# The first 256 tokens of a max-of-three layer begun while the attention of the next 256 is prepared

## The chip, the cores and the metric

One core of a Trainium2 chip runs the kernel. The engines are TensorE (PE; its weight loads are listed apart as PEld), VectorE (DVE), ScalarE (ACT), GpSimd (POOL) and SyncE (SP, which here issues most of the DMAs). The metric is the device time of one launch in microseconds (us), the median of several runs.

## The reference

Linear attention with a decay per step feeds a layer that takes the largest of three products and multiplies by a fourth matrix. Four batches, 8 heads, 768 steps, head size 48; 3072 tokens, model width 384, inner width 768.

```python
def _attn_ref(r, k, v, w, u):
    state = np.zeros((B, H, D, D)); y = np.zeros_like(r)
    for t in range(S):
        cur = np.einsum('bhd,bhe->bhde', u[None] * kt, vt)
        y[:, :, t] = np.einsum('bhd,bhde->bhe', rt, state + cur)
        state = wt[:, :, :, None] * state + np.einsum('bhd,bhe->bhde', kt, vt)
    return y

def _moe_ref(x, w1, w2, w3, w_out):
    h = np.maximum(np.maximum(x @ w1, x @ w2), x @ w3)
    return h @ w_out
```

## The kernel before

The attention runs in 24 chunks of 128 steps, numbered through the batches, six to a batch. The layer runs in six halves of 512 tokens, so four chunks feed one half. The steps of a chunk k have one letter each, and a table of such letters sets the order in which they are written into the engines' queues; every engine then works strictly in that order, and waits with everything behind it when an operand is missing.

- **b, f**: two scans on DVE over the decays (L324, L334); two short operations stand ahead of f (L332, L333). **r**: two multiplications on DVE that apply the scans to the keys and queries in `tin` (L345, L344). **c**: a check on ACT.
- **d, e**: the diagonal term of the first eight chunks: a multiplication on DVE into `kr` (L356), four small products on PE (L369, written as part of e), a copy of their sums to SBUF on DVE (`cs`, L371), and a select on POOL that spreads them into `a` (L376).
- **X**: the scores on PE (L394). **M**: two masked copies on DVE that take the scores into `a` (L401). **T**: transposes on PE (L411), copied by ACT into `kn`.
- **R, V**: products on PE with the state (L424) and the values (L458) into `y`. **E**: ACT copies `y` into `x` (L467). **U**: products on PE for the next state (L434, for chunks 1 to 3 also L438). **S**: its scaling on DVE (L449).
- **n**: the load of `tin` of a chunk (SP). **w**: the load of one of the 24 weight tiles (SP). **W**: products on zeros on PE, which have no reader (L490).

After E of the last chunk of a half, six small DMAs copy rows inside `x` (L472), three from each of SP and ACT for half 0, and six from SP for the later halves. Only then can the half's products start. The weights arrive in 64 bits and are turned into fp32 by one ACT operation (L268) and two on DVE (L277, L279) for each of the 24 tiles, the "conversion" below. Half 0 is "plain": it multiplies fp32 tiles as they are. The later halves split `x` and the weights into two parts and make three products of each.

A half has 18 column groups, three (one of each weight matrix) for each 128 columns of the inner width. A group is three 128x512 matmuls in PSUM (L146). ACT copies the first of three groups to SBUF, and DVE takes the maximum with the second and third (L128). The string `START` sets how groups (m), attention steps (a), conversions (c) and splits (f) alternate until half 1 begins; after that a rule in the main loop does. Every DMA issue waits until the one eight issues earlier has landed.

Of the kernel before, what the change touches and what calls it, by code (L numbers as in the profile page):

```python
# [42 lines left out]
NP = 4  # L43
# [23 lines left out]
FRONT = "w U0 b1 | d1 f1 r1 | w e1 c1 S0 W2 X1 T1 | R0 M0 | V0 E0 n3 |"  # L67
LAST = "w R0 M0 | V0 E0 U0 W9 n3 | b1 d1 | f1 r1 w | e1 c1 S0 X1 T1 R1 |"
TURN = "b1 d1 w | f1 w | r1 c1 | e1 M0 w | "
ORD = "w R0 X1 U0 V0 E0 b2 d2 | f2 n3 w | S0 r2 c2 | e2 M1 w | T1 w | |"  # L70


START = ("aaaaaaaaaaaacaaacaccaxmcacmcamcamcamcamcamcamcamcaamca"
         "mcmacamcacammacmcamacamcamcamcamcamcaafafafaxmafmmammaaf")
# [15 lines left out]
def kernel(ctx: ExitStack, tc, tin, nat, u_flat, u_pair, v_t, w_all, out, ytr):  # L90
# [21 lines left out]

    def moe_groups(x_hi, x_lo, pools, store):

        plain = x_lo is None
        ps_m, hp, mp = pools
        h_hi, h_lo, later, behind = [], [], [], []
        top = {}  # L120

        def take_up(wi, ps):
            if wi == 0:
                top["m"] = hp.tile([128, HT], F32, name="h_hi") if plain else mp.tile([128, HT], F32, name="m")
                nc.scalar.copy(out=top["m"][:, :], in_=ps[:, :])
                return
            m = top["m"]
            nc.vector.tensor_tensor(out=m[:, :], in0=ps[:, :], in1=m[:, :], op=ALU.max)  # L128
            if wi == 2 and plain:
                h_hi.append(m)  # L130
            elif wi == 2:
# [20 lines left out]
        flush(behind)  # L152
        flush(later)
        order = []
        for tt in range(CPH):
            order += [(tt, f) for f in range(FT - 1)]
            order += [(tt - 1, FT - 1)] if tt else []
        order.append((CPH - 1, FT - 1))
        pss = {}
        for n, (tt, f) in enumerate(order):  # L160
            if f == 0:
                pss[tt] = ps_m.tile([128, HT], F32, name="psm")
# [12 lines left out]
    with ExitStack() as fast:  # L175
# [23 lines left out]
        def load_nat(k):  # L199
            b, c = divmod(k, NCH)  # L200
            vt = v_p.tile([128, DM], F32, name="v")
            kr = nat_p.tile([128, 2, DM], F32, name="kr")
            if k >= CS:
                nc.sync.dma_start(out=kr[:, :, :], in_=nat[b, c, :, 1:3, :])
            nc.sync.dma_start(out=vt[:, :], in_=nat[b, c, :, 0, :])
            natt[k] = (vt, kr)
# [108 lines left out]
        load(1)  # L315
        load(2)
        u_bc = cst.tile([128, DM], F32, name="u_bc")
# [34 lines left out]
        def prep_diag1(k):  # L352
            n = natt[k][1]
            if k < CS:
                t = tbuf[k % NB]
                nc.vector.tensor_tensor(out=n[0:112, :, :].rearrange("p a b -> p (a b)")[:, 0:NP * C],  # L356
                                        in0=t[0:112, WC:WC + NP * C], in1=t[0:112, WC + NP * C:TC_], op=ALU.mult)
                return
            nc.gpsimd.tensor_tensor(out=n[:, 0, :], in0=n[:, 0, :], in1=n[:, 1, :], op=ALU.mult)
            nc.gpsimd.tensor_tensor(out=n[:, 0, :], in0=n[:, 0, :], in1=u_bc[:, :], op=ALU.mult)  # L360

        def prep_diag2(k):
            n = natt[k][1]
            cs = small.tile([128, LINE], F32, name="cs")[:, 0:H]
            if k < CS:
                t = tbuf[k % NB]
                ps = ps_m.tile([128, HT], F32, name="psm")
                for pr in range(NP):
                    nc.tensor.matmul(ps[:, 2 * pr:2 * pr + 2], lhsT=n[0:112, :, :].rearrange("p a b -> p (a b)")[:, pr * C:(pr + 1) * C],  # L369
                                     rhs=t[0:112, TC_ + 2 * pr:TC_ + 2 * pr + 2], start=(pr == 0), stop=(pr == NP - 1))  # L370
                nc.vector.tensor_copy(out=cs[:, :], in_=ps[:, 0:H])  # L371
            else:
                nc.vector.tensor_reduce(out=cs[:, :], in_=n[:, 0, :].rearrange("p (h d) -> p h d", h=H),  # L373
                                        axis=AX.X, op=ALU.add)
# [10 lines left out]
        def scores(k):  # L385

            p = prep[k]
            spare = k < CPH and k % 2
            p["gs"] = gs = [ps_m.tile([128, NP, C], F32, name="psm") if spare else ps_g.tile([128, NP, C], F32, name="gram")
                            for _ in range(2)]  # L390
# [70 lines left out]
        def result(k):  # L461
# [12 lines left out]
        steps = dict(X=scores, M=take, T=transposes, R=from_state, U=to_state, S=state, V=values, E=result, n=load,  # L474
                     b=prep_scan_b, f=prep_scan_f, r=prep_rk, c=prep_check, d=prep_diag1, e=prep_diag2)
# [11 lines left out]
        def warmer(n):  # L487
            wps = ps_m.tile([128, HT], F32, name="psm")
            for _ in range(n):
                nc.tensor.matmul(wps[:, :], lhsT=warm[:, :], start=True, stop=True,  # L490
                                 rhs=warm[:, :].unsqueeze(1).broadcast_to([128, HT // 128, 128]))

        def attn():
            for step in "bdfeWrXTcW":
                ahead(step, 0) if step != "W" else warmer(2 if ("X", 0) in ready else 8)
            for k in range(NK):
                if k == CPH:
                    nc.scalar.dma_start(out=u_bc[:, :], in_=u_flat.partition_broadcast(128))
                for step in (FRONT if k < CPH - 1 else LAST if k < CPH else TURN + ORD if k == CPH else ORD).split():
# [4 lines left out]
                    elif step[0] == "W":  # L504
                        warmer(int(step[1]))
                    else:
                        ahead(step[0], k + int(step[1]))

        def x_parts(half):
            x = xt.pop(half)  # L510
            if half < PLAIN:
                return x, None
# [14 lines left out]
        done = fixed = 0  # L527

        def weights():

            nonlocal done
            if done > NW:
                return
            while loaded < min(NW, done + NST):
                load_w()
            if done < NW:
                split_w1(done)
            if done >= 1:
                split_w2(done - 1)
# [13 lines left out]
        units = groups = 0  # L553
# [34 lines left out]

        def group():
            nonlocal groups, mg  # L590
            half = groups // GPH
            if groups % GPH == 0:
# [3 lines left out]

                def store(tt, o):
                    nc.sync.dma_start(out=out[half * HT + tt * C:half * HT + (tt + 1) * C, :], in_=o)

                mg = moe_groups(*xs[half], pools, store)  # L600
            g = groups % GPH
            while done < 1 + (NW if half or g >= 3 * FT else g + 1):
# [10 lines left out]

        for step in START:
            if step == "a":
                unit()
            elif step == "c":
                weights()
# [4 lines left out]
            else:  # L623
                group()
# [163 lines left out]
```

## Time and profile before

| | us |
|---|---|
| median of three runs | 432.44 (430.42 to 436.3) |
| the profiled execution, its own time | 429.81 |
| span of its trace | 428.1 |

The trace covers 428.1 us of the profiled execution's 429.81 us. In the trace PE is the engine with the longest busy time, and nearly all of its idle time lies in the first 40 us. A fp32 matmul stands in the trace as two PE instructions.

### The profile page before, as it was taken

How to read it: one execution, taken by the hardware profiler on the slowest of the kernel's cores; microseconds unless marked ns; L12 is line 12 of the kernel's file. 1: busy time of each engine (PE TensorE's matmuls, PEld its weight loads, DVE VectorE, ACT ScalarE, POOL GpSimd, SP SyncE). 2: the span in 40 equal slices, each digit the busy share in tenths (PEclk: the TensorE clock that was granted, in tenths of full speed). 3: DMA queues.
4: the chain of work that ended last, by engine and by line, in shares of the span. 5: the costliest groups of instructions: out<-in, count | busy, mean ns of one | idle time of the engine just before them, and what ended most of it. 6: DMA issues, size and time to landing. Idle time of an engine off the chain costs nothing.

```text
span 428.1 us, 7355 instructions
## 1 busy us (share of the span) xinstructions
PE 414.1 (97%) x2921; PEld 324.8 (76%) x2921; DVE 275.6 (64%) x483; ACT 152.4 (36%) x318; POOL 64.4 (15%) x67
## 2 busy tenths in 40 slices
PE   6998999999999999999999999999999999999994
PEld 2774555546678888988888978888988888988893
DVE  6999779788759968747758458758547623233310
ACT  1353424142534534425334445434623321312211
POOL 3120111030333021112103112202112100000000
PEclk9899999999999999999999999999999999999998
DMA  8868935443280412294643494662360000200001
GB/s 218 262 183 246 319 88 167 115 144 93 67 255 13 122 39 83 48 311 161 195 147 122 143 314 140 190 195 75 103 231 2 0 2 2 93 2 0 1 21 61
DMA packets 20701, 53.22 MB, mean 124 GB/s; under 512 B 2816, under 2 KB 9088, under 8 KB 20656
## 3 DMA queue, kind: packets, MB, share of 16 engines
q1 hardware_dynamic: 16832, 42.61, 32.6%
q10 hardware_dynamic: 3824, 10.03, 7.5%
q8 instruction: 25, 0.41, 0.4%
q14 instruction: 20, 0.16, 0.1%
HBM read 46.74 MB, written 4.72 MB: 120 GB/s over the span
## 4 chain that ended last, share of the span: by engine, by line
PE 93%; DMA 3%; DVE 1%; ACT 1%; issue 1%; SPq 0%; DVEq 0%; ACTq 0%
PE psm L146 55%; PE psm L166 18%; PE y L458 6%; PE gram L394 5%; PE y L424 3%; PE tu L434 2%; PE tu L411 2%; DMA tin<-in_tin_dram 2%; PE psm L369 1%; DMA x<-x 1%; PE psm L394 1%; DVE x_lo L106 0%; DVE gf L334 0%; DVE gf L324 0%; ACT x L467 0%
## 5 line engine op out<-in xcount | busy, mean ns | idle before, releaser
L146 PE MATMUL psm<-x_hi,w 128*128 128x512 f32 x540 | 172.9, 394 | 0.0
L146 PEld LDWEIGHTS psm<-x_hi,w 128*128 128x128 f32 x540 | 101.4, 188 | 22.7 <-issue 2.1
L146 PE MATMUL psm<-x_lo,w 128*128 128x512 f32 x270 | 105.3, 390 | 0.0
L128 DVE TENSOR_TENSOR m<-psm,m 128x512 f32<-128x512 f32 x60 | 41.2, 687 | 59.6 <-PE psm L146 52.7
L166 PE MATMUL psm<-w,h_hi 128*128 128x384 f32 x288 | 78.1, 364 | 0.0
L376 POOL TENSOR_SCALAR_AFFINE_SELECT a<-cs 128x1024 f32<-128x1024 f32 x24 | 26.7, 1111 | 245.6 <-DVE cs L373 153.8
L146 PEld LDWEIGHTS psm<-x_lo,w 128*128 128x128 f32 x270 | 50.7, 188 | 10.2 <-DVE x_lo L106 0.2
L166 PEld LDWEIGHTS psm<-w,h_hi 128*128 128x128 f32 x288 | 51.8, 188 | 7.0 <-issue 1.0
L146 PE MATMUL psm<-x,w 128*128 128x512 f32 x108 | 48.3, 598 | 2.1 <-DMA x<-x 2.1
L467 ACT COPY x<-y 112x512 f32<-112x512 f32 x24 | 14.1, 587 | 77.7 <-PE y L458 77.7
L166 PE MATMUL psm<-w,h_lo 128*128 128x384 f32 x120 | 40.2, 335 | 0.0
L105 ACT CAST h_hi<-m 128x512 fp32r<-128x512 f32 x30 | 18.7, 622 | 57.6 <-DVE m L128 57.2
L146 PEld LDWEIGHTS psm<-x,w 128*128 128x128 f32 x108 | 19.9, 190 | 25.0 <-issue 22.0
L350 ACT ACTIVATE gf<-gf 112x1034 f32<-112x1034 f32 x24 | 25.6, 1069 | 34.1 <-DVE tin L345 31.4
L106 DVE TENSOR_TENSOR h_lo<-m,h_hi 128x512 fp32r<-128x512 f32 x30 | 21.9, 732 | 21.4 <-ACT h_hi L105 21.4
L324 DVE TENSOR_TENSOR_SCAN gf<-tin,d_bwd 112x517 f32<-112x517 f32 x24 | 29.5, 1228 | 7.3 <-DMA tin<-in_tin_dram 7.3
L334 DVE TENSOR_TENSOR_SCAN gf<-tin,d_fwd 112x517 f32<-112x517 f32 x24 | 29.6, 1235 | 0.8
L401 DVE COPY_PREDICATED a<-mask,gram 128x512 f32<-128x512 int32 x44 | 30.0, 736 | 0.0
L458 PE MATMUL y<-a,v 128*48 128x128 f32 (+1 forms) x384 | 27.8, 281 | 0.0
L394 PE MATMUL gram<-tin 48*128 48x128 f32 x352 | 25.6, 284 | 0.9 <-DVE tin L345 0.9
L394 PEld LDWEIGHTS gram<-tin 48*128 48x128 f32 x352 | 21.4, 187 | 6.7 <-issue 4.1
L458 PEld LDWEIGHTS y<-a,v 128*64 128x64 f32 (+1 forms) x384 | 22.2, 133 | 1.3 <-issue 0.8
(71 smaller groups left out, 420.2 us busy)
## 6 DMA issues: line engine op xcount, KB each, us to landing
tin<-in_tin_dram SPq DMA_DIRECT2D x23, 677.7 KB, 5.5
w<-in_w_all_dram SPq DMA_DIRECT2D x24, 384.0 KB, 7.7
cv<-in_w_all_dram ACTq DMA_DIRECT2D x24, 384.0 KB, 3.2
kr<-in_nat_dram SPq DMA_DIRECT2D x16, 384.0 KB, 5.7
v<-in_nat_dram SPq DMA_DIRECT2D x24, 192.0 KB, 5.2
out_dram<-m SPq DMA_DIRECT2D x24, 192.0 KB, 2.7
x<-x SPq DMA_DIRECT2D x33, 32.0 KB, 2.0
tin<-in_tin_dram SPq DMA_DIRECT2D x1, 258.0 KB, 4.4
```

What stands on the lines that cost most here:

```text
L105: nc.scalar.copy(out=hi, in_=src)
L106: rest = lambda: nc.vector.tensor_tensor(out=lo, in0=src, in1=hi.bitcast(F32), op=ALU.subtract)
L128: nc.vector.tensor_tensor(out=m[:, :], in0=ps[:, :], in1=m[:, :], op=ALU.max)
L146: nc.tensor.matmul(ps[:, :], lhsT=wt[f * 3 + wi][:, ct * 128:(ct + 1) * 128], rhs=xt[:, ct, :], start=(n == 0), stop=(n == KT * len(terms) ...
L166: nc.tensor.matmul(pss[tt][:, 0:DM], lhsT=ht[f][:, tok], rhs=wt[FT * 3 + f][:, :], start=(f == 0 and i == 0), stop=(f == FT - 1 and i == l ...
L324: nc.vector.tensor_tensor_scan(out=gf[0:112, 0, ::-1], data0=t[0:112, 0:WC][:, ::-1], data1=d_bwd[0:112, ::-1], initial=0.0, op0=ALU.mult, ...
L334: nc.vector.tensor_tensor_scan(out=gf[0:112, 1, :], data0=tbuf[k % NB][0:112, 0:WC], data1=d_fwd[0:112, :], initial=0.0, op0=ALU.mult, op1 ...
L350: nc.scalar.activation(out=flat, in_=flat, func=AF.Square, accum_out=acc[0:112, k:k + 1])
L376: nc.gpsimd.affine_select(out=a[:, :, :], in_=cs[:, :].unsqueeze(2).broadcast_to([128, H, C]), pattern=[[0, H], [1, C]], compare_op=ALU.is ...
L394: nc.tensor.matmul(gs[hh][:, pr, :], lhsT=p["kp"][q:q + 48, pr, :], rhs=p["rp"][q:q + 48, pr, :], start=(pr == 0), stop=(pr == NP - 1))
L401: nc.vector.copy_predicated(out=p["a"][:, hh::2, :], mask=mask_b(NP), data=p["gs"][hh][:, :, :])
L458: nc.tensor.matmul(p["y"][64 * half:64 * half + m, hh, j, :], lhsT=natt[k][0][:, h * D:h * D + m], rhs=p["a"][:, h, :], start=(k % NCH == ...
```

## The change

A new table `FRONT`, written out step by step with chunk numbers, replaces the tables `FRONT` and `LAST` and the beginning of `START`. It covers everything up to chunk 4.

- E of chunk 1 now starts six copies inside `x` for the first 256 tokens, three from SP and three from ACT. E of chunk 3 starts six for the other 256, all from SP.
- The nine groups of the first 384 inner columns run twice on 256 tokens (token `g` for the first time) instead of once on 512. They need chunks 0 and 1 alone.
- The conversion has two halves that the table places apart (`i` for ACT's part, `c` for both).
- The four small products of the diagonal term are a step of their own (D), and the scores of chunks 1 and 3 use the same PSUM pool as the others.
- In the front, a maximum is put into DVE's queue when the table says so (`u`) or when the third PSUM tile after it is taken; after the front, as before, one group later.
- The second chunk's values and four weight tiles are loaded earlier; products on zeros stand at other places (29 instead of 35).

The order below `START` differs until half 1 has begun; from its fifth group on PE's order is what it was.

```diff
-FRONT = "w U0 b1 | d1 f1 r1 | w e1 c1 S0 W2 X1 T1 | R0 M0 | V0 E0 n3 |"
+FRONT = ("b0 d0 D0 W6 f0 r0 X0 e0 T0 W2 c0 b1 M0 U0 R0 V0 E0 n3 i i d1 D1 W6 S0 f1 r1 e1 X1 c1 T1 R1 i "
...
+START = ("mmacmmacmmacmmacmaacmacmaacmacmaacmacmaacmacmacmaacmaacmaafxmafmmafmmaaf")
+EARLY = 3
...
+    def take_turn(pool):
+        rules["turns"] += 1
+        while held and held[0][0] <= rules["turns"] - 3:
+            held.pop(0)[1]()
+        return pool.tile([128, HT], F32, name="psm")
...
-        for f in range(FT):
+        whole, first, second = slice(0, HT), slice(0, HT // 2), slice(HT // 2, HT)
+        stretches = [(f, whole) for f in range(FT)]
+        if plain:
+            stretches = [(f, first) for f in range(EARLY)] + [(f, second if f < EARLY else whole) for f in range(FT)]
+        for f, cols in stretches:
             for wi in range(3):
                 flush(later)
-                ps = ps_m.tile([128, HT], F32, name="psm")
+                ps = take_turn(ps_m)
...
-                        nc.tensor.matmul(ps[:, :], lhsT=wt[f * 3 + wi][:, ct * 128:(ct + 1) * 128], rhs=xt[:, ct, :],
+                        nc.tensor.matmul(ps[:, cols], lhsT=wt[f * 3 + wi][:, ct * 128:(ct + 1) * 128], rhs=xt[:, ct, cols],
                                          start=(n == 0), stop=(n == KT * len(terms) - 1))
                         n += 1
-                flush(behind)
-                behind.append(lambda wi=wi, ps=ps: take_up(wi, ps))
+                while held and not rules["lazy"]:
+                    held.pop(0)[1]()
+                held.append((rules["turns"], lambda f=f, wi=wi, ps=ps, cols=cols: take_up(f, wi, ps, cols)))
                 yield
...
-            for lo in (0, 64) if slot == CPH - 1 else ():
-                for j in range(KT):
-                    eng = nc.scalar if lo and half < PLAIN else nc.sync
-                    eng.dma_start(out=x[lo + 48:lo + 64, j, :], in_=x[lo + 16 * j:lo + 16 * j + 16, KT, :])
+            early = half < PLAIN and slot == CPH // 2 - 1
+            cols = slice(HT // 2 if half < PLAIN and not early else 0, HT // 2 if early else HT)
+            for j in range(KT) if early or slot == CPH - 1 else ():
+                for lo in (0, 64):
+                    eng = nc.scalar if lo and early else nc.sync
+                    eng.dma_start(out=x[lo + 48:lo + 64, j, cols], in_=x[lo + 16 * j:lo + 16 * j + 16, KT, cols])
...
+        def early_group():
+            nonlocal ahead_by
+            if ahead_by == 0:
+                xs[0] = x_parts(0)
+                begin_half(0)
+            while done < ahead_by + 1:
+                weights()
+            next(mg)
+            ahead_by += 1
```

Three places show what moved. The first is PE where the layer starts. Names: `warm` are the zeros, `psm` a PSUM tile, `tin_114` to `tin_116` the three buffers of `tin` (chunk modulo 3). Before:

```order
L490 LDWEIGHTS warm
L490 MATMUL psm<-warm 128x512
L146 MATMUL psm<-x,w 128x512 x9
L369 MATMUL psm<-tin_115,kr 128x2 x4
L394 MATMUL gram<-tin_115 128x128 x8
L411 MATMUL tu<-ident,tin_115 128x112 x4
```

After:

```order
L520 LDWEIGHTS warm
L520 MATMUL psm<-warm 128x512
L162 MATMUL psm<-x,w 128x256 x3
L393 MATMUL psm<-tin_116,kr 128x2 x4
L162 MATMUL psm<-x,w 128x256 x6
L421 MATMUL gram<-tin_116 128x128 x8
L438 MATMUL tu<-ident,tin_116 128x112 x4
```

Before, the layer's products stand behind chunk 3 and ahead of chunk 4; now the first three groups stand ahead of the scores of chunk 2.

The second is DVE between the first scan of chunk 2 and its second. Before:

```order
L324 SCALAR_TENSOR_TENSOR gf<-tin_116,d_bwd 112x517
L356 TENSOR_TENSOR kr<-tin_116 112x512
L332 TENSOR_SCALAR d_fwd<-gf 112x4
L333 RECIPROCAL d_fwd<-d_fwd 112x4
L334 SCALAR_TENSOR_TENSOR gf<-tin_116,d_fwd 112x517
```

After:

```order
L350 SCALAR_TENSOR_TENSOR gf<-tin_116,d_bwd 112x517
L428 COPY_PREDICATED a<-mask,gram 128x4x128 x2
L298 SCALAR_TENSOR_TENSOR cv<-w,cv 128x384
L300 SCALAR_TENSOR_TENSOR w<-w,cv 128x384
L298 SCALAR_TENSOR_TENSOR cv<-w,cv 128x384
L300 SCALAR_TENSOR_TENSOR w<-w,cv 128x384
L298 SCALAR_TENSOR_TENSOR cv<-w,cv 128x384
L300 SCALAR_TENSOR_TENSOR w<-w,cv 128x384
L382 TENSOR_TENSOR kr<-tin_116 112x512
L476 TENSOR_TENSOR sstar_134<-tu,dec_136 112x4x48
L358 TENSOR_SCALAR d_fwd<-gf 112x4
```

Chunk 1's scores are now taken inside chunk 2's preparation, and three conversions stand ahead of the rest of it.

The third is SP's queue, from the load of chunk 3 on (`tin_114` for the second time). Before:

```order
L216 DMA tin_114<-in_tin_dram 112x1549
L252 DMA w<-in_w_all_dram 128x384 x2
L205 DMA v<-in_nat_dram 128x384
L216 DMA tin_115<-in_tin_dram 112x1549
L252 DMA w<-in_w_all_dram 128x384 x2
```

After:

```order
L237 DMA tin_114<-in_tin_dram 112x1549
L273 DMA w<-in_w_all_dram 128x384
L501 DMA x<-x 16x256 x3
L273 DMA w<-in_w_all_dram 128x384 x2
L237 DMA tin_115<-in_tin_dram 112x1549
```

The early copies inside `x` now stand behind one load of `tin` and one of a weight, and ahead of the next loads.

## Rows read from the trace of the kernel before

**Rows 1.** The page's busy time of PE over the span, and PE's busy tenths in 40 slices of the span.

```profile
PE 414.1 (97%) x2921; PEld 324.8 (76%) x2921; DVE 275.6 (64%) x483; ACT 152.4 (36%) x318; POOL 64.4 (15%) x67
PE   6998999999999999999999999999999999999994
```

**Rows 2.** Busy time by stretch: start and end, length, then busy us (and instructions) of PE, PEld, DVE, ACT and POOL, TensorE's granted clock, DMA share and GB/s.

```profile
0.00:38.24 38.24, 30.76 (x330) 21.64 (x330) 33.01 (x61) 14.29 (x28) 6.56 (x15) 0.96 0.77 218
38.24:421.30 383.06, 382.87 (x2591) 303.04 (x2592) 242.62 (x424) 137.12 (x288) 57.82 (x52) 1.00 0.37 116
```

**Rows 3.** The chain of work that ended last, from 0 to 140 us: start, length, engine and line. From 22.14 on it passes through chunk 2 and the diagonal term of chunk 3; at 99.36 it is in the second product of half 0 (128x384 matmuls).

```profile
22.14 1.09 PE gram L394 x16
23.23 0.54 PE tu L411 x4
23.77 0.59 PE y L424 x10
24.36 1.02 PE y L458 x15
25.38 0.45 PE tu L434 x15
25.83 0.51 PE tu L438 x2
26.34 0.79 PE psm L369 x8
...
33.34 0.59 ACT x L467
...
33.95 4.20 DMA x<-x
...
38.24 7.96 PE psm L146 x18
...
99.36 7.94 PE psm L166 x24
```

**Rows 4.** DVE in order of time: start, busy us, what. The first is chunk 0, the second chunk 1, then chunk 3 and one conversion, then the first maximum of the layer.

```profile
8.81 1.58 DVE L345 TENSOR_TENSOR tin<-tin,gf 112x512 f32<-112x512 f32 x1
10.55 1.24 DVE L324 TENSOR_TENSOR_SCAN gf<-tin,d_bwd 112x517 f32<-112x517 f32 x1 [0.16 <-DMA tin<-in_tin_dram]
...
22.92 1.23 DVE L324 TENSOR_TENSOR_SCAN gf<-tin,d_bwd 112x517 f32<-112x517 f32 x1
24.06 0.68 DVE L356 TENSOR_TENSOR kr<-tin 112x512 f32<-112x512 f32 x1
...
25.07 1.23 DVE L334 TENSOR_TENSOR_SCAN gf<-tin,d_fwd 112x517 f32<-112x517 f32 x1
26.22 0.67 DVE L344 TENSOR_TENSOR tin<-tin,gf 112x512 f32<-112x512 f32 x1
...
27.40 0.16 DVE L371 COPY cs<-psm 128x8 f32<-128x8 f32 x1
27.48 0.35 DVE L449 TENSOR_TENSOR sstar<-tu,dec 112x192 f32<-112x192 f32 x1
27.74 1.36 DVE L401 COPY_PREDICATED a<-mask,gram 128x512 f32<-128x512 int32 x2
28.98 0.55 DVE L277 SCALAR_TENSOR_TENSOR cv<-w,cv 128x384 uint32<-128x384 uint32 x1
...
30.08 1.33 DVE L401 COPY_PREDICATED a<-mask,psm 128x512 f32<-128x512 int32 x2
...
43.73 0.69 DVE L128 TENSOR_TENSOR h_hi<-psm,h_hi 128x512 f32<-128x512 f32 x1 [1.66 <-PE psm L146]
44.34 0.55 DVE L277 SCALAR_TENSOR_TENSOR cv<-w,cv 128x384 uint32<-128x384 uint32 x1
```

**Rows 5.** PE's weight loads of the plain half, from the page's groups by line (busy us, mean ns, idle before).

```profile
L146 PEld LDWEIGHTS psm<-x,w 128*128 128x128 f32 x108 | 19.9, 190 | 25.0 <-issue 22.0
```

**Rows 6.** DMA issues: what, queue, number, size of one, median us from issue to landing. The weights are those of the first 60 us, the first two copies inside `x` those of 33.9 to 36.1 us, the third all that SP issued in the span.

```profile
w<-in_w_all_dram SPq DMA_DIRECT2D x17, 384.0 KB, 8.2
...
x<-x SPq DMA_DIRECT2D x3, 32.0 KB, 3.7
x<-x ACTq DMA_DIRECT2D x3, 32.0 KB, 3.9
...
x<-x SPq DMA_DIRECT2D x33, 32.0 KB, 2.0
```

**Rows 7.** SP's issues in order of time, the six copies of half 1: start, time from the first issue to the end of the last.

```profile
111.51 3.68 SPq L472 DMA_DIRECT2D x<-x  x6
```

**Rows 8.** Stretches as in Rows 2: one in which the granted clock is low, the wait ahead of the layer's first product, and what follows it.

```profile
15.70:19.10 3.40, 3.40 (x30) 2.90 (x28) 3.33 (x7) 1.21 (x3) 0.66 (x1) 0.51 0.97 274
36.19:38.24 2.05, 0.00 (x1) 0.03 (x1) 2.02 (x5) 1.27 (x3) 0.00 (x0) 1.00 0.65 158
38.24:41.60 3.36, 3.36 (x8) 1.59 (x9) 3.26 (x8) 0.51 (x2) 0.00 (x0) 1.00 0.97 273
```

**Rows 9.** Stretches as in Rows 2, in the first product of half 0.

```profile
38.24:50.00 11.76, 11.76 (x64) 6.62 (x65) 8.38 (x17) 3.92 (x7) 1.09 (x1) 1.00 0.97 325
50.00:60.00 10.00, 10.00 (x28) 4.64 (x27) 8.27 (x15) 3.85 (x8) 0.00 (x0) 1.00 0.69 190
60.00:70.00 10.00, 10.00 (x69) 5.68 (x69) 9.30 (x18) 2.22 (x6) 1.09 (x1) 1.00 0.30 86
```

More of the change, by code (lines that the diff above doesn't have):

```diff
@@ L118, in moe_groups, with take_up @@
         ps_m, hp, mp = pools
[L119 removed]
+        h_hi, h_lo, later = [], [], []
         top = {}
[L122 removed]
+        def take_up(f, wi, ps, cols):
             if wi == 0:
[L124 to L131 removed]
+                if f not in top:
+                    top[f] = hp.tile([128, HT], F32, name="h_hi") if plain else mp.tile([128, HT], F32, name="m")
+                    if plain:
+                        h_hi.append(top[f])
+                nc.scalar.copy(out=top[f][:, cols], in_=ps[:, cols])
+                return
+            m = top[f]
+            nc.vector.tensor_tensor(out=m[:, cols], in0=ps[:, cols], in1=m[:, cols], op=ALU.max)
+            if wi == 2 and not plain:
                 hi = hp.tile([128, HT], F32R, name="h_hi")
@@ L315 @@
         load(1)
+        load_nat(1)
         load(2)
+        for _ in range(3):
+            load_w()
+        load_nat(2)
+        load_w()
         u_bc = cst.tile([128, DM], F32, name="u_bc")
@@ L387, in scores @@
             p = prep[k]
-            spare = k < CPH and k % 2
-            p["gs"] = gs = [ps_m.tile([128, NP, C], F32, name="psm") if spare else ps_g.tile([128, NP, C], F32, name="gram")
-                            for _ in range(2)]
+            p["gs"] = gs = [ps_g.tile([128, NP, C], F32, name="gram") for _ in range(2)]
             for pr in range(NP):
@@ L493, in attn @@
         def attn():
[L494 to L499, printed above, removed]
+            nc.scalar.dma_start(out=u_bc[:, :], in_=u_flat.partition_broadcast(128))
+            for k in range(CPH, NK):
+                for step in (TURN + ORD if k == CPH else ORD).split():
                     if step == "|":
@@ L526, with begin @@
         at = attn()
-        done = fixed = 0
+        begun = done = fixed = 0
+        def begin():
+            nonlocal begun
+            while loaded < min(NW, begun + NST):
+                load_w()
+            if begun < NW:
+                split_w1(begun)
+                begun += 1
         def weights():
             nonlocal done
-            if done > NW:
+            if done == NW:
                 return
[L534 to L539, printed above, removed]
+            while begun < min(NW, done + 2):
+                begin()
+            split_w2(done)
             done += 1
@@ L552 @@
         warmer(WARM)
-        units = groups = 0
+        units, groups, ahead_by = UPH - 4, 0, 0
         xs, mg = {}, None
@@ L587, in take_x, with begin_half, store @@
                 xs[h] = x_parts(h)
+        def begin_half(half):
+            nonlocal mg
+            def store(tt, o):
+                nc.sync.dma_start(out=out[half * HT + tt * C:half * HT + (tt + 1) * C, :], in_=o)
+            mg = moe_groups(*xs[half], pools, store)
+        def early_group():
[7 more added lines that the diff above has]
+            ahead_by += 1
         def group():
-            nonlocal groups, mg
+            nonlocal groups
             half = groups // GPH
-            if groups % GPH == 0:
+            assert ahead_by == 3 * EARLY
+            if groups % GPH == 0 and half:
                 while half not in xs:
@@ L595, in group @@
                     take_x()
-                def store(tt, o):
-                    nc.sync.dma_start(out=out[half * HT + tt * C:half * HT + (tt + 1) * C, :], in_=o)
-                mg = moe_groups(*xs[half], pools, store)
+                begin_half(half)
             g = groups % GPH
-            while done < 1 + (NW if half or g >= 3 * FT else g + 1):
+            while done < (NW if half or g >= 3 * FT else g + 1):
                 weights()
@@ L612, in group @@
                     fetch_w()
+        simple = dict(c=weights, i=begin, g=early_group, w=load_w, m=group, u=lambda: held.pop(0)[1]())
+        rules["lazy"] = True
+        for step in FRONT.split():
+            if step in simple:
+                simple[step]()
+            elif step[0] == "W":
+                warmer(int(step[1:]))
+            else:
+                ahead(step[0], int(step[1:]))
+        rules["lazy"] = False
         for step in START:
@@ L623 @@
             else:
-                group()
+                simple[step]()
         while groups < GPH * NH:
```

56 lines of the change are left out of this document (29 added, 27 removed), and 3 rows, old and new, of the table FRONT.

## The prediction

> **What bounds the kernel now.** I read the share of each engine first, then PE by stretch, then the chain through the first 40 us. PE is busy for 97% of the span, and the slices below nine tenths are the first ones and the last [rows 1]. By stretch, PE is idle for 7.5 of the first 38.24 us and for 0.2 of the 383 that follow [rows 2]. So from 38.24 us on the end is the sum of PE's work, and a change of order gains only what it takes out of the front. Most of the front's busy time is no gain either, since products on zeros count as busy. What counts is PE's useful work there. One chunk costs, by the spacing in the chain: D 0.79, X 1.09, T 0.54, R 0.59, V 1.02, U 0.45 and 0.51 [rows 3], 4.99 us together; chunk 0 has no R and no second U and costs 3.89. Chunks 0 to 3 are 3.89 + 3 x 4.99 = 18.9 us. The other 38.24 - 18.9 = **19.3 us** of the front are waits and zeros.
>
> **What could be won.** The early groups fill that time, but they can't start before chunk 1 has its result and its copies, and PE then also waits for DVE. So I walk both queues up to the place where PE is dense again, and count what is done there.
>
> Durations. On DVE I take the spacing of neighbours in a full stretch [rows 4]: first scan 1.14 (22.92 to 24.06); multiplication into `kr`, the two short ones 1.01 (to 25.07); second scan 1.15; the two multiplications of r 1.18; `cs` 0.08; state 0.26; take 1.24; one conversion 1.10 (28.98 to 30.08). A maximum over 512 columns is 0.61 (43.73 to 44.34); one over 256 isn't in the trace, and I take 0.34, halfway between that and the 0.08 of the 8 columns of `cs`. An early group is six PE instructions over 256 columns. Over 512 one is 7.96/18 = 0.442, over 384 it is 7.94/24 = 0.331 [rows 3]; the line through both gives 0.221 for 256, still above the 0.190 of a weight load [rows 5]. So a group is 1.33 us, two of them are 2.66 instead of 2.65 for the whole, and running nine groups twice costs **0.1 us**. Were the loads not hidden at all, the 54 added instructions would cost 54 x 0.19 = 10 us; I leave that end out of the range, as the smaller products of the attention (16 instructions of X in 1.09 us) show loads of this size hidden to a large part.
>
> First stretch, to the first early product. Chunk 1's first scan starts at 10.55, when its load lands [rows 4]; that load keeps its place in SP's queue, and what is moved stands behind it, so I change nothing. Then take of chunk 0 (11.7 to 12.9), `kr`, short ones and state (to 14.2), second scan (15.35), r (16.5), `cs`, first scan of chunk 2 (17.75), take of chunk 1 to 19.0. PE runs V to 20.05, ACT copies the result in 0.59, and the copies inside `x` go out at 20.7. From first issue to last landing three and three took 4.20 [rows 3]; they land at 24.9, and the first product starts at **25.0**. At that point PE has done chunks 0 and 1, 8.9 us; 16.1 are already lost.
>
> Second stretch. PE: group 1 to 26.3, D of chunk 2 27.1, groups 2 and 3 29.8, X, T, R of chunk 2 32.0, group 4 33.35, V and U 35.3, group 5 36.65, D of chunk 3 37.45, group 6 38.8. DVE beside it: three conversions after the take bring it to 22.3, it prepares chunk 2 to 25.9, then waits for D, which now stands behind group 1: `cs` 27.2, scan of chunk 3 28.3, the two maxima of groups 2 and 3 to 30.15, fourth conversion 31.25, take of chunk 2 32.5, fifth conversion 33.6, `kr` 34.2, a wait for U to 35.3, state, sixth conversion 36.7, second scan and r to 39.45, `cs` and a scan 40.65, take of chunk 3 41.9. So X of chunk 3 waits for r (0.65 of idle PE) and V for the take (0.25): X, T, R to 41.7, V to 42.95, U to 43.9. The second copies go out at 43.6. Six from one queue need 3.68 to issue [rows 7], and the last lands some 2.0 [rows 6] after its own start: 48.7. Under them PE has groups 7, 8, D of chunk 4 and group 9 from 43.9 to 48.7, for which DVE's conversions (44.8, 45.9) and `kr` (46.5) are just in time. The copies cost nothing while that cover holds, and any further delay of them in full.
>
> Sum. At 48.7 PE has done 18.9 + 9 x 1.33 + 0.79 = 31.6 us of useful work; 17.1 are lost, against 19.3. Less the 0.1 the gain is **2.1 us**.
>
> The rest. From 48.7 on the work is that of before. DVE has to keep up with a PE some 2 us earlier; it was busy for 8.4, 8.3 and 9.3 of the next three stretches [rows 9], 5.8 us of air, and walking on I find PE waiting nowhere; at the edge to half 1, 15 second products now stand behind chunk 7's V where 12 stood. The loads behind the second copies stand still on SP from about 33 to 47; the weight next in line is converted near 65, which leaves twice the 8.2 that a weight took to land [rows 6]. Fewer zeros (29 for 35) and the moved maxima cost nothing where PE or DVE waits anyway.
>
> The profiled execution would go from 429.81 to 427.7. The median of the runs shown lies 2.6 above it; on that scale 432.44 - 2.1 is **430.3**. Under 2%, 8.6 us, a measurement of this kernel can hardly tell from no change.
>
> **A rule against the change.** PE's clock stood at 0.51 from 15.7 to 19.1 though PE was busy throughout, and at 1.00 in the 3.36 us after the wait of 2.05 us ahead of the first product [rows 8]. In the new front PE waits from about 22.2 (the last zeros) to 25.0, longer than that. The page TensorE: Matmul & The Clock Gate of the Trainium skill, section HAM oscillation, says that a wait for a DMA between bursts of matmuls throws the array back to half rate, so that the next burst starts cold. By that rule the early groups begin at 1.2 GHz; by the second row they keep 2.4 GHz.
>
> **The rivals.**
>
> *The clock falls ahead of the early groups.* For it: a wait of 2.8 us, and a fall in this front already. Against it: the wait of 2.05 cost nothing. Price as in the low stretch: 3.4 us at 0.51 lose 1.7. Gain 0.4, 432.0.
>
> *The early copies land later (slower than before).* They are issued behind a load of `tin` and one of a weight that SP sent some 8 us earlier, and wherever in the front weights were loaded they took 8.2 in the median, against 3.7 and 3.9 for the copies [rows 6]. PE has nothing ahead of D of chunk 2 but group 1, so each us of delay is one of the end, and the gain is gone when they land at 27.0. If the last one, issued at 22.1, takes 8.2, they land at 30.3: 5.4 later, a loss of 3.3, 435.7. Against it: in the kernel before, a load of `tin` and one of a weight stood ahead of the copies too.
>
> *They land sooner.* The later copies took 2.0 [rows 6], with the queues emptier. Then the first product, which needs two of the six, could start at 22.9 and the group end at 24.6 instead of 26.3: 1.7 more, 428.6. Against it: by the volume issued the queues are full until about 22.
>
> *DVE is late.* From 28 to 46 it has next to no idle time in my walk, and everything on PE hangs on it. One multiplication took 1.58 instead of 0.68 beside a select on POOL [rows 4]; two such cost 1.8: 432.1.
>
> **How the numbers follow.** My forecast 0.52 (its own range 429.3 to 431.3, the landing one us either way), clock 0.16, DVE late 0.10, copies sooner 0.10, copies later 0.08, anything else 0.04. The first three hold 0.78 within 429 to 432.5; with part of the sooner and the later landings, and the spread of 430.4 to 436.3 that three runs of one kernel show, the range is 427 to 434.5. Faster by over 2% would need 8.6 of the 19.3 us, though 16.1 are lost before the first early product: 0.04. Slower by over 2% needs the late copies and another mishap: 0.03.
>
> **What would show it.** PE's first 128x256 product near 25; chunk 3's X and V a little late, behind DVE; the second halves starting near 48.7 without a wait; PE dense afterwards with the same order of sums. I am wrong if PE waits again between 50 and 120, if the granted clock is near 0.5 after 25, or if the early groups take clearly more than 1.33 us.

## The result: slower by 1.3%

The changed kernel takes **437.05 us** (median of four runs, 435.26 to 437.7), the kernel before, in the same turn, 431.8. The ratio is 1.0132, interval 1.0098 to 1.0165. 430.3 was forecast, with a range to 434.5: a small gain was promised and a clear loss came. The profiled execution takes 437.7, its span is 435.9; before it was 428.1, so 7.8 us are to be found.

### The profile after

The page: span, busy time, PE's busy tenths and granted clock in 40 slices (against [rows 1]).

```profile
span 435.9 us, 7474 instructions
PE 416.1 (95%) x2969; PEld 332.5 (76%) x2969; DVE 273.6 (63%) x489; ACT 151.9 (35%) x321; POOL 66.1 (15%) x67
PE   6898999998989999999999999999999999999994
PEclk9999999999999999999999999999999999999998
```

PE's share falls from 97 to 95%. The thin slices are no longer the first ones alone: there are eights up to slice 12, which ends at 131 us. PE's waits by releaser (total us, times, longest) name them; in [rows 2] PE had 0.2 us of idle time behind 38.24.

```profile
PE tu L438 <- DVE sstar L476: 1.9, 1, 1.9
PE y L485 <- DVE a L428: 1.7, 5, 0.6
PE gram L421 <- DVE tin L371: 1.6, 3, 0.8
PE psm L184 <- ACT m L188: 1.5, 1, 1.5
PE psm L162 <- ACT h_hi L139: 1.3, 1, 1.3
```

The y and gram waits lie in the preparation. The other three stand alone, at 66, 107 and 121 us, where PE was to be dense. After them the two kernels run alike: the transposes of chunk 9, at the same place of PE's order, start at 134.69 before and at 142.18 after (next two fences), which is 7.5 of the 7.8.

```profile
134.69 0.55 PE L411 MATMUL tu<-ident,tin 112*128 112x112 f32 x4
```

```profile
142.18 0.55 PE L438 MATMUL tu<-ident,tin 112*128 112x112 f32 x4
```

**The preparation.** PE in order of time (start, us, line, shape, count, idle time ahead and its releaser): the first early group, chunk 3's X and V, the ninth early group with the first second half.

```profile
24.30 1.96 PE L162 MATMUL psm<-x,w 128*128 128x256 f32 x6 [0.81 <-DVE kr L382]
...
39.76 1.16 PE L421 MATMUL gram<-tin 48*128 48x128 f32 x16 [0.84 <-DVE tin L371]
...
42.62 0.43 PE L485 MATMUL y<-a,v 128*64 128x128 f32 x4 [0.58 <-DVE a L428]
...
49.11 2.84 PE L162 MATMUL psm<-x,w 128*128 128x256 f32 x12
```

The early work starts at 24.30 (25.0 forecast), X of chunk 3 at 39.76 (39.45). The releaser named ahead of the first group is only the nearest in time, since the group doesn't read `kr`: the first pair of copies inside `x` was issued at 22.1 and landed 1.8 and 2.0 us later. The first second half is the last six of the twelve from 49.11, so it starts near 50.5; 48.7 was forecast. By the prediction's count 31.6 us of useful work are done there, so some 18.8 are lost, against 19.3 in the kernel before. The front gains some 0.5, not 2.2.

**The three waits, link by link.** At 66: ScalarE's queue, then PE.

```profile
64.08 1.07 ACT L376 ACTIVATE gf<-gf 112x1034 f32<-112x1034 f32 x1 [4.88 <-DVE tin L371]
65.05 0.18 ACT L376 ACTIVATION_READ_ACCUMULATOR gf<-gf 112x1 f32 x1
65.14 0.62 ACT L289 ACTIVATE cv<-w,minus_two 128x384 f32<-128x384 uint32 x1
65.67 0.35 ACT L139 COPY h_hi<-psm 128x256 f32<-128x256 f32 x1
```

```profile
66.07 1.13 PE L162 MATMUL psm<-x,w 128*128 128x256 f32 x4 [1.31 <-ACT h_hi L139]
```

The 0.35 us copy frees PE's PSUM tile. It stands behind chunk 5's check, and ScalarE idles 4.88 us ahead of that check until VectorE has multiplied r. At 107 the chain runs through three engines (ACT, DVE, PE):

```profile
101.30 0.59 ACT L494 COPY x<-y 112x512 f32<-112x512 f32 x1 [5.66 <-PE y L485]
101.78 0.20 ACT L352 COPY dec<-gf 112x4 f32<-112x4 f32 x1
101.88 1.19 ACT L289 ACTIVATE cv<-w,minus_two 128x384 f32<-128x384 uint32 x2
```

```profile
102.56 0.56 DVE L298 SCALAR_TENSOR_TENSOR cv<-w,cv 128x384 uint32<-128x384 uint32 x1 [3.48 <-ACT cv L289]
```

```profile
107.25 0.61 PE L438 MATMUL tu<-ident,tin 112*128 112x112 f32 x4 [1.92 <-DVE sstar L476]
```

ScalarE's part of two conversions stands behind chunk 6's result copy, which waits 5.66 us for PE's V. VectorE idles 3.48 us for the conversion, is late with the state behind it, and PE waits 1.92 us. Then the granted clock falls (stretch, length, busy us of PE, PEld, DVE, ACT, POOL, clock, DMA share, GB/s):

```profile
108.00:112.00 4.00, 4.00 (x22) 1.79 (x21) 3.23 (x5) 1.58 (x3) 3.01 (x2) 0.61 0.00 0
```

Four microseconds at 0.61 are 1.6 us lost. At 121 a copy of the second product that frees PSUM stands behind the three casts of the next half's x, each of which waits for its copies inside `x`:

```profile
117.91 0.62 ACT L107 CAST x_hi<-x 128x512 fp32r<-128x512 f32 x1 [2.11 <-DMA x<-x]
119.16 0.62 ACT L107 CAST x_hi<-x 128x512 fp32r<-128x512 f32 x1 [0.63 <-DMA x<-x]
120.44 0.62 ACT L107 CAST x_hi<-x 128x512 fp32r<-128x512 f32 x1 [0.66 <-DMA x<-x]
120.97 0.47 ACT L188 COPY m<-psm 128x384 f32<-128x384 f32 x1
```

PE's wait for it is the 1.5 of `psm L184 <- ACT m L188` above. Sum to chunk 9: 1.3 + 1.9 + 1.6 + 1.5 = 6.3 lost in three places, 0.5 won in the front; about 1.7 of the 7.5 these rows put to no place. Idle time understates the waits, since the end of a matmul in the profile is modelled and runs past the start of the next: in the single records of the trace PE's starts are 1.69, 2.41 and 1.96 apart at the three waits, where 0.22, 0.32 and 0.32 are usual. That makes 5.2 of the 4.7, and about 1.2 stay open.

### The profile page after: what moved, and what is told of

Read it like the earlier page. It is cut to its first block, busy times and chain, and to the rows that moved or that the text cites. A ratio compares the mean times of both kernels' runs of the same rounds, so it can differ in the third digit from the quotient of the medians.

```text
span 435.9 us, 7474 instructions
## 1 busy us (share of the span) xinstructions
PE 416.1 (95%) x2969; PEld 332.5 (76%) x2969; DVE 273.6 (63%) x489; ACT 151.9 (35%) x321; POOL 66.1 (15%) x67
## 4 chain that ended last, share of the span: by engine, by line
PE 82%; DVE 7%; ACT 2%; issue 2%; DMA 2%; POOL 1%; SPq 1%; DVEq 0%; ACTq 0%; POOLq 0%
PE psm L162 51%; PE psm L184 15%; PE gram L421 5%; PE y L485 5%; PE y L451 2%; PE tu L461 2%; PE tu L438 2%; POOL a L405 1%; DVE gf L360 1%; DMA tin<-in_tin_dram 1%; DVE cv L298 1%; SPq L501 1%; DMA x<-x 1%; PE psm L393 1%; DVE kr L382 1%
## 5 line engine op out<-in xcount | busy, mean ns | idle before, releaser
L162 PE MATMUL psm<-x_hi,w 128*128 128x512 f32 x540 | 172.6, 394 | 0.1
L162 PEld LDWEIGHTS psm<-x_hi,w 128*128 128x128 f32 x540 | 101.3, 188 | 22.9 <-issue 2.1
L162 PE MATMUL psm<-x_lo,w 128*128 128x512 f32 x270 | 105.2, 390 | 0.0
L184 PE MATMUL psm<-w,h_hi 128*128 128x384 f32 x288 | 80.1, 371 | 1.5 <-ACT m L188 1.5
L405 POOL TENSOR_SCALAR_AFFINE_SELECT a<-cs 128x1024 f32<-128x1024 f32 x24 | 29.6, 1234 | 247.4 <-DVE cs L402 156.5
L184 PEld LDWEIGHTS psm<-w,h_hi 128*128 128x128 f32 x288 | 52.4, 191 | 9.6 <-issue 2.2
L162 PEld LDWEIGHTS psm<-x_lo,w 128*128 128x128 f32 x270 | 50.7, 188 | 9.9
L162 PE MATMUL psm<-x,w 128*128 128x256 f32 (+1 forms) x162 | 50.7, 459 | 2.3 <-ACT h_hi L139 1.3
L162 PEld LDWEIGHTS psm<-x,w 128*128 128x128 f32 x162 | 29.4, 190 | 17.2 <-issue 11.5
L184 PE MATMUL psm<-w,h_lo 128*128 128x384 f32 x120 | 40.2, 335 | 0.0
L428 DVE COPY_PREDICATED a<-mask,gram 128x512 f32<-128x512 int32 x48 | 32.7, 738 | 2.8 <-POOL a L405 2.8
L421 PEld LDWEIGHTS gram<-tin 48*128 48x128 f32 x384 | 23.3, 187 | 8.5 <-issue 4.4
L421 PE MATMUL gram<-tin 48*128 48x128 f32 x384 | 27.9, 284 | 1.6 <-DVE tin L371 1.6
L108 DVE TENSOR_TENSOR x_lo<-x,x_hi 128x512 fp32r<-128x512 f32 x15 | 9.8, 689 | 25.7 <-ACT x_hi L107 25.7
```

Of the source, the lines that this page charges most:

```text
L108: rest = lambda: nc.vector.tensor_tensor(out=lo, in0=src, in1=hi.bitcast(F32), op=ALU.subtract)
L162: nc.tensor.matmul(ps[:, cols], lhsT=wt[f * 3 + wi][:, ct * 128:(ct + 1) * 128], rhs=xt[:, ct, cols], start=(n == 0), stop=(n == KT * len( ...
L405: nc.gpsimd.affine_select(out=a[:, :, :], in_=cs[:, :].unsqueeze(2).broadcast_to([128, H, C]), pattern=[[0, H], [1, C]], compare_op=ALU.is ...
L421: nc.tensor.matmul(gs[hh][:, pr, :], lhsT=p["kp"][q:q + 48, pr, :], rhs=p["rp"][q:q + 48, pr, :], start=(pr == 0), stop=(pr == NP - 1))
L428: nc.vector.copy_predicated(out=p["a"][:, hh::2, :], mask=mask_b(NP), data=p["gs"][hh][:, :, :])
```

## The experiments

All start from the changed kernel. In its strings `m` is a group of the layer, `a` the next steps of the attention, `c` a whole conversion, `i` ScalarE's part of one, `x` the splitting of the next half's x.

### Is it VectorE's order in the preparation?

```diff
-FRONT = "... f0 r0 X0 e0 ... f1 r1 e1 X1 ... f3 r3 e3 X3 ..."
+FRONT = "... f0 e0 r0 X0 ... f1 e1 r1 X1 ... f3 e3 r3 X3 ..."
```

> The changed kernel with one thing moved: for chunks 0, 1 and 3 DVE copies cs, which releases the select on POOL, ahead of the two multiplications of r instead of behind them and right ahead of a scan. PE, ACT, POOL and SP keep their order. Theory: beside a scan the select takes 1.96 us instead of 1.1, the take waits 0.92 for it, three times, twice ahead of the first early product. Expected: takes of chunks 0, 1 and 3 without a wait, first early product near 22.5 instead of 24.3, 1.8 to 2.7 us faster than the changed kernel (433 to 434 us by its median of 437.05). Rival: what follows is set by the order of PE and ACT, and the time given back here is lost again at the three later waits of PE: under 0.5 us, 436.5 or more.

Measured: 437.6 us (435.69 to 442.2): no gain, the rival's number. In the profiled execution X of chunk 0 took 2.08 us, against 1.16 in the changed kernel, so its times can't be set beside that kernel's, and only two durations are read from it, of POOL's select and of VectorE's second multiplication:

```profile
19.58 1.48 POOL L405 TENSOR_SCALAR_AFFINE_SELECT a<-cs 128x1024 f32<-128x1024 f32 x1 [8.65 <-DVE cs L400]
```

```profile
20.03 1.58 DVE L371 TENSOR_TENSOR tin<-tin,gf 112x512 f32<-112x512 f32 x1
```

The select no longer takes 1.96 beside a scan, but 1.48, and the multiplication beside it goes from 0.69 to 1.58. The contention moved, it didn't go, and r, for which X waits, came later. Whether that alone cost the gain isn't shown.

### The three late waits, one by one

Each edit moves only ScalarE's queue. PE's order is that of the changed kernel in all three.

```diff
-TURN = "... | D1 r1 c1 | e1 M0 w | "
+TURN = "... | D1 r1 | e1 M0 c1 w | "
```

> The changed kernel with the check of chunk 5 moved behind two conversions and one copy of a group in ACT's queue, nothing else. Theory: PE's wait of 1.31 us at 64.8 is the copy that frees its PSUM tile, which stood on ACT behind a check that waits for DVE's multiplications. Expected: this wait gone, 1.3 us faster than the changed kernel, about 435.7. Rival: PE then waits at the same place for DVE's maximum or conversion, since DVE is the one that is late there: at most 0.4 us faster.

Measured: 435.02 (433.5 to 436.62), 2.0 below the changed kernel, for 1.3 expected; `psm L162 <- ACT h_hi L139` is gone from PE's waits.

```diff
-START = "...macmacmaacmaacmaafx..."
+START = "...macmiiacmaacmaacmaafx..."
```

> The changed kernel with ACT's part of the last two conversions moved ahead of the copy of chunk 6's result in ACT's queue, nothing else. Theory: DVE waits 3.48 us for these conversions, because ACT waits for PE's V of chunk 6 first, so the state scaling is late and PE's transposes of chunk 7 wait 1.92 us; the granted clock then is 0.61 over the next 4 us, some 1.6 to 1.8 more. Expected: wait and low clock both gone, 3.5 us faster, about 433.5. Rival: the clock falls anyway or the wait moves to the next product: 0 to 1.9 us faster.

Measured: 433.17 (432.79 to 434.5), 3.9 below. The wait of 1.9 is gone, and so is the low clock:

```profile
108.00:112.00 4.00, 4.00 (x60) 3.15 (x53) 0.00 (x0) 1.09 (x3) 1.35 (x2) 1.00 0.00 0
```

```diff
-START = "...maafxmafmmafmmaaf"
+START = "...maafmmxafmafmmaaf"
```

> The changed kernel with the casts of half 1's tokens moved behind the copy of the first output tile in ACT's queue, nothing else. Theory: PE's wait of 1.48 us at 120 is for that copy, which frees a PSUM tile and stood on ACT behind casts that wait for the copies inside x. Expected: this wait gone, 1.5 us faster than the changed kernel, about 435.5. Rival: half 1's first product then comes sooner than its split tokens and waits instead: 0 us.

Measured: 435.61 (434.12 to 436.44), 1.4 below. PE's waits, and the stretch in which the clock had fallen:

```profile
PE tu L438 <- DVE sstar L476: 1.9, 1, 1.9
...
PE psm L162 <- ACT m L188: 0.7, 1, 0.7
```

```profile
108.00:112.00 4.00, 3.85 (x39) 2.61 (x41) 4.00 (x7) 1.58 (x3) 2.11 (x2) 1.00 0.01 4
```

By the rows the move is worth 0.8: the wait of 1.5 leaves, and one of 0.7 comes, of the next half's first product for the same engine. And the clock didn't fall in this execution, although PE waited the 1.9 us as before: the wait alone doesn't decide the fall. The mean granted clocks of all executions agree. It is 0.992 to 0.994 in two of four of the changed kernel, six of ten with the first edit and two of ten with this one, and 0.995 or more in all the others and in all ten with the second edit, which takes the wait away. With the first edit the two kinds lie 2 us apart (435.0 to 436.6 and 433.5 to 433.9), so part of each difference of medians is this chance.

### The three together, and what is left

The three diffs in one kernel:

> The three edits to ScalarE's queue of the last call together (chunk 5's check behind the copy, the two weight conversions ahead of chunk 6's result copy, the output copy ahead of the x_hi casts); VectorE's queue is that of the changed kernel, TensorE's order is the same. Theory (the loss is these waits, each by itself): the gains add up, 2.0 + 3.9 + 1.4 = 7.3 us off 437.05, so 429.7 us, which is the time of the kernel before within 0.4%. Rival (a wait that goes only makes the next step late, and something else holds the layer back in that stretch): less than half of the sum, 433.4 us or more, with new waits of TensorE between 60 and 130 us.

Measured: **430.97 us** (430.5 to 432.05), 1.0013 of the kernel before (0.9993 to 1.0032). The gain is 6.1 of the 7.3 that the sum of the medians gives, and with 0.8 for the third, as its rows say, of 6.7. What PE still waits for behind 50 us is 0.8 for `m L188` and pieces of 0.2. By the ratios to the kernel before in the same turn (1.0132 for the changed kernel, then 1.0087, 1.0070, 1.0097, and 1.0013 together) the parts are 1.9, 2.7 and 1.5 and the whole 5.1 us, again five sixths of the sum. So the three waits, with the low clock behind one of them, are most of the loss.

That the rest is nothing doesn't follow, for the kernel before has more executions with a low clock. In this turn nine of its runs have a mean clock of 0.994 or more and took 428.7 to 430.0 us, median 429.4; its other runs, but for one of 436.4, have 0.988 to 0.991 and took 430.4 to 432.6. All twelve of this kernel have 0.994 or more. At like clock it is some 1.5 us slower than the kernel before. On top of the three edits, chunk 5's scan ahead of the maximum:

```diff
-START = "mmacmmac..."
+START = "ammcmmac..."
```

> As e5, and chunk 5's first scan and its product k times r stand on VectorE ahead of the maximum for which VectorE idles 3.87 us at 51.9 us. Theory: once ScalarE's copies are free nobody waits for VectorE there, so VectorE's idle time costs nothing: 0 to 0.5 us below e5. Rival (VectorE's lateness after 52 us is the root, and ScalarE's copies only its last link): 1.5 us or more below e5, and the TensorE waits that e5 still has get shorter.

Measured: 430.47 (430.1 to 431.69), 0.5 below e5 (the kernel with the three edits), which is less than the spread of the runs: the first theory. VectorE's idle 3.87 us cost next to nothing once ScalarE's copy was free.

### What the select beside a scan costs

```diff
-FRONT = "... T1 R1 i b2 M1 V1 E1 ..."
+FRONT = "... T1 R1 i M1 b2 V1 E1 ..."
```

> As e5, and chunk 2's first scan stands on VectorE behind chunk 1's two takes instead of ahead of them, so that VectorE does nothing while GpSimd's selection of chunk 1 runs. Theory (the selection is held up by the scan beside it): the selection falls from 1.96 to about 1.1 us, the takes and with them the result of chunk 1 and the first early product come about 0.85 us earlier (23.4 instead of 24.3 us), while chunk 2's scan ends about 0.4 us later or not at all, so the layer gains 0.3 to 0.8 us. Rival (the selection is slow for another reason, such as its operand or its place): it stays near 1.9 us and the first early product comes no earlier or later.

Measured: 430.63 (429.73 to 431.71), 0.3 below e5, again within the spread. Chunk 1 in the changed kernel (scan, take; select), then in this one (`cs`, take; select):

```profile
17.05 1.22 DVE L350 TENSOR_TENSOR_SCAN gf<-tin,d_bwd 112x517 f32<-112x517 f32 x1
19.19 1.33 DVE L428 COPY_PREDICATED a<-mask,gram 128x512 f32<-128x512 int32 x2 [0.92 <-POOL a L405]
```

```profile
17.20 1.96 POOL L405 TENSOR_SCALAR_AFFINE_SELECT a<-cs 128x1024 f32<-128x1024 f32 x1 [5.14 <-DVE cs L400]
```

```profile
17.84 0.16 DVE L400 COPY cs<-psm 128x8 f32<-128x8 f32 x1
19.24 1.36 DVE L428 COPY_PREDICATED a<-mask,gram 128x512 f32<-128x512 int32 x2 [1.24 <-PE gram L421]
```

```profile
18.06 1.09 POOL L405 TENSOR_SCALAR_AFFINE_SELECT a<-cs 128x1024 f32<-128x1024 f32 x1 [6.52 <-DVE cs L400]
```

Beside the scan the select takes 1.96, alone 1.09, while the scan takes its 1.22 either way. This execution ran later from the start (X of chunk 0 took 1.42 us for 1.16), so times are counted from `cs`: the take starts 0.8 us earlier (1.40 for 2.22 us), and the first early product 0.5 (24.64 - 17.84 = 6.80 for 24.30 - 16.97 = 7.33). The other 0.3 went in ScalarE's queue, where the copy of chunk 1's result stands behind one that waits for the scan that was moved:

```profile
21.75 0.20 ACT L352 COPY dec<-gf 112x4 f32<-112x4 f32 x1 [0.96 <-DVE gf L350]
21.85 0.58 ACT L494 COPY x<-y 112x512 f32<-112x512 f32 x1
```

### What the early groups and the zeros are worth

First the changed kernel with its early groups left out: the layer begins with whole groups.

```diff
-EARLY = 3
+EARLY = 0
-FRONT = "... W5 g d2 D2 g S1 g i ... u u ... g ..."
+FRONT = "... W5 d2 D2 S1 i ..."
```

> The changed kernel without its early column groups: the nine products on 256 tokens are left out of the preparation of chunks 2 and 3, and the layer begins with whole groups on 512 tokens as before; the new order of loads, steps and zeros stays. The 54 instructions took 12.0 us of TensorE. Theory (they filled waits, but made the preparation longer): the x copies are issued 3 to 5 us earlier than 44.8 us, so 7 to 9 of the 12 us have to be found again: 442 to 447 us less what the later waits give back, 439 to 446. Rival (the early groups bring nothing, since the preparation is stretched by as much as they fill): 437 us or less.

Measured: **448.75** (448.08 to 450.26), 11.7 above the changed kernel and above the theory's 446, too: left out, the groups cost nearly all of their 12.0 us. The first whole group starts where the second halves started. That the groups don't lengthen the preparation isn't shown by this, since without them the clock falls to half (stretches of 24 to 50.5 us):

```profile
50.45 4.51 PE L162 MATMUL psm<-x,w 128*128 128x512 f32 x6
```

```profile
24.00:38.00 14.00, 8.86 (x86) 7.80 (x86) 12.49 (x24) 4.54 (x9) 2.41 (x1) 0.71 0.94 280
38.00:50.50 12.50, 9.48 (x79) 8.03 (x79) 8.70 (x18) 3.98 (x8) 1.90 (x1) 0.50 0.24 70
```

So the new order without its filling, at this clock, starts the layer at 50 instead of 38 us, and the groups pay that back and little more. Are VectorE's conversions the reason? The next kernel also leaves the nine conversions of the preparation and their loads for the layer:

```diff
-FRONT = "... w w n4 v3 c c c W5 ... n5 c M2 ... c d3 S2 c D3 ... c c c d4 ..."
+FRONT = "... w w n4 v3 W5 ... n5 M2 ... d3 S2 D3 ... d4 ..."
```

> As e8 (448.75, no early groups), and the nine weight conversions of the preparation (18 instructions of VectorE of 0.55, 10 us together) and their loads are left for the first whole groups, as in the kernel before. Theory (the conversions on VectorE are what makes the preparation long in the new order): the first whole group starts near 41 us instead of 50.45 and the time is 438 to 441. Rival (they stand in waits of VectorE, and the low clock or the order of the steps stretches the preparation): it starts at 47 us or later and the time is 445 or more.

Measured: 450.87 (450.31 to 451.52): the rival's numbers, but in another way. Chunk 3's takes start at 37.31 instead of the 40.86 of the kernel above, 3.5 us earlier and not 9; then the first group waits for its own conversion and starts at 47.63:

```profile
47.63 4.77 PE L162 MATMUL psm<-x,w 128*128 128x512 f32 x6 [4.62 <-DVE w L300]
```

The granted clock was 0.79 and 0.66 from 24 to 40 us here, too, so how the long preparation divides between conversions, clock and order stays open. The zeros by themselves, on the kernel of e5:

```diff
-FRONT = "b0 d0 D0 W6 f0 ... T0 W2 c0 ... D1 W6 S0 ... W5 g ..."
+FRONT = "b0 d0 D0 f0 ... T0 c0 ... D1 S0 ... g ..."
```

> As e5 (430.97), without the products on zeros inside the preparation (6, 2, 6 and 5 of them, ahead of 25 us; the ten at the very start stay). Theory (they keep TensorE's granted clock up while VectorE works): without them the clock is near 0.5 from about 8 us to the first early products, the products of chunks 0 and 1 take twice as long (X 2.1 for 1.1, V 2.0 for 1.0, T, U and D likewise), about 4 us of that on the path to chunk 1's result: first early product near 27.5 us, time 433.5 to 436. Rival (TensorE works hardly on the path there, VectorE sets it): the first early product within 1 us of e5's 23.8 and the time within 1 us of 431.0.

Measured: 435.73 (433.54 to 437.54), 4.8 above e5: the time of the first theory. The first early product came at 25.36, not at 27.5, and the rest was lost behind it:

```profile
25.36 2.90 PE L162 MATMUL psm<-x,w 128*128 128x256 f32 x6 [1.11 <-DVE d_fwd L359]
```

```profile
8.00:16.00 8.00, 5.90 (x53) 5.00 (x53) 6.21 (x12) 1.68 (x5) 1.09 (x1) 0.59 1.04 348
16.00:24.00 8.00, 7.03 (x78) 5.73 (x78) 6.98 (x14) 4.45 (x9) 1.96 (x1) 0.71 0.42 117
24.00:32.00 8.00, 6.89 (x21) 5.68 (x21) 4.93 (x10) 1.54 (x3) 1.89 (x1) 0.50 0.75 224
```

With the zeros the clock was 1.00 in the first 24 us of the changed kernel and of e5. They don't ensure it: in the execution of the first experiment X of chunk 0, right behind zeros, took 2.08 us for 1.16. The section HAM oscillation, in the Trainium skill's page TensorE: Matmul & The Clock Gate, tells of bursts that each start cold behind a wait for a DMA. No run here shows that for the early groups: without the zeros they ran at 0.50, but the clock had been at 0.50 already from 19.6 to 24.2 us, ahead of their wait; in the changed kernel, whose PE waited 0.81 us, they ran at 1.00.

### The moves put together

The three edits of e5, chunk 5's scan ahead of the maximum (e6), chunk 1's behind the takes (e7), chunk 4's scan behind chunk 3's takes, and the output copy ahead of chunk 8's check:

```diff
-FRONT = "... T3 R3 b4 M3 V3 ..."
+FRONT = "... T3 R3 M3 b4 V3 ..."
-START = "...maafmmxafmafmmaaf"
+START = "...maafmmxmafafmmaaf"
```

> The three moves of e5 with chunk 5's scan ahead of the maximum (e6) and the scan behind the takes for chunk 1 (e7) and for chunk 3 as well; the output copy also goes ahead of chunk 8's check. Theory (each move is worth its wait: e6 0.5, e7 0.35, chunk 3's takes 0.3 to 0.8, the output copy up to 0.8): 429.0 to 429.8 us, 0.3 to 0.5% below the kernel before. Rival (with TensorE at 95% and more the small waits no longer add up): 430.3 us or more, as e6 and e7 alone.

Measured: **429.52** (429.2 to 430.98), 0.9973 of the kernel before (0.9945 to 1.0001). It is 1.4 below e5 and in the middle of what was expected; that it beats the kernel before isn't shown, the interval just holds 1. And what lies below 1 is the clock: all twelve executions have a mean of 0.995 or more, and the eight of the kernel before in this turn with 0.993 or more took 428.4 to 430.4 us, median 429.1. The output copy's move gained nothing: PE's 0.8 for `m L188` stayed.

POOL's selects of chunks 0, 1 and 3 all take 1.09 here, and V of chunk 3 waits no more. Still the ninth early group starts only 0.6 earlier than in e5 (47.98 for 48.59), and 0.5 of that was there at the first (23.27 for 23.79). What chunk 3 gave, groups 7 and 8 lose to VectorE's conversions:

```profile
43.55 1.56 PE L162 MATMUL psm<-x,w 128*128 128x256 f32 x6 [0.33 <-DVE w L300]
45.41 1.56 PE L162 MATMUL psm<-x,w 128*128 128x256 f32 x6 [0.29 <-DVE w L300]
```

## Why the prediction was wrong

**The step that failed** is "walking on I find PE waiting nowhere". Behind 48.7 I walked PE and VectorE and counted VectorE's busy time. ScalarE, busy a third of the span, I didn't walk. Its queue is in order, and the changed strings put copies that free PSUM, and first parts of conversions, behind instructions that wait: for r, for V, for copies inside `x`. Three such places make 4.7 us of waits and, in the profiled execution, 1.6 of low clock. The test I had set ("if PE waits again between 50 and 120") is the one that failed. The three edits to that queue alone take 6.1 us off by the medians, 5.1 by the ratios.

**The front gained 0.5 instead of 2.2.** In the walk takes followed as if POOL's select were ready. It took 1.9 to 2.0 beside the next chunk's scan, and the takes of chunks 0, 1 and 3 waited 0.9 us each. I had the 1.58 beside a multiplication in front of me [rows 4] and made a rival of it at 1.8 us; the scan, the neighbour that the new order gives, wasn't in the trace of before. That the front fell 1.7 short, near the 1.8 of that rival, is luck: the multiplications kept 0.69, and it was the select that grew. Up to D of chunk 3 PE was even a little ahead of the walk (36.56 for 36.65). X of chunk 3 then came 0.3 late, the end of its U 1.0 (44.91 for 43.9), and the second halves 1.8. With all three selects at 1.09 (the last kernel) 0.6 came back. The rest is not divided; at least the conversions of groups 7 and 8, "just in time" in the walk, are then the next to be late.

**The early copies landed 1.8 to 2.1 us after issue, not the 3.7 and 3.9 of [rows 6]**: the sooner rival came true, and hid the late takes. They were issued 1.4 late (22.1 for 20.7), so two errors cancel by luck: the early groups began at 24.3 for 25.0, D of chunk 2 at 26.1 for 26.3. The 4.20 of the walk was misread, too: in the kernel before it is the time to the landing of the first pair, which the first product waited for; the last of the six landed at 38.8, 4.8 after the first issue.

**The clock** was 1.00 from 24.3 to 30 us, against the clock rival. But that rival's condition, a wait of 2.8 us, didn't come: zeros kept PE busy to 23.5, and it waited 0.81. The clock fell at another place, behind the wait at 107 us, that the prediction hadn't looked at.

**Right:** the price of a narrow group (30 instructions in 6.74 us in e5, 0.224 each, for 0.221), and with it that running them twice costs next to nothing; the maxima over 256 columns (0.42 busy, 0.34 apart); and that the second copies cost nothing under the ninth group. That the early groups fill time which would else be lost is confirmed (11.7 us without them); what they would be worth at a clock that holds without them isn't shown.

## What to carry to other kernels

Walk every in-order queue past the edit, the least busy engine's too: what counts there is who frees a buffer, and behind which waiting instruction it stands. Work that fills waits is worth its full length only if the order that makes room for it costs nothing; test the order without the filling, and read the clock in that test, since here it fell to 0.50 when the filling was gone. When a regression has several waits, move one instruction of the queue that releases each: here three short edits found most of it. And where the granted clock differs between executions, compare those of like clock before a gain of some tenths of a per cent is believed.

## What the runs showed of the hardware

- A select on POOL takes 1.09 us alone, 1.48 beside multiplications with two SBUF inputs (one of which goes from 0.69 to 1.58), and 1.96 beside a scan, which itself keeps its 1.22.
- After the same wait of 1.9 us at the same place the granted clock of 108 to 112 us was 0.61 in one execution, 0.66 in another (the first of the three edits) and 1.00 in a third (the third of the edits).
- Copies of 16 KB inside SBUF landed 1.8 to 2.1 us after issue when the loads ahead of them were through (DMA share 0.09 from 22.0 to 24.3 us). Those of 32 KB took 3.7 and 3.9 beside loads (DMA share 0.65 and more from 33.95 to 38.2 us in the kernel before) and 2.0 later [rows 6].
